# Turning eight probability tiles in float32 instead of as two float16 parts

## The chip, the cores and the metric

One core of a Trainium2 chip. The metric is the device time of one execution in microseconds, as the median over runs.

## The reference

Three layers follow each other, for 2 batches of 768 positions. All inputs are float32.

```python
# 1: attention inside hash buckets, 8 heads of 64
mask = q_bucket[:, :, :, None] == k_bucket[:, :, None, :]
scores = np.where(mask, scale * np.matmul(q, k.transpose(0, 1, 3, 2)), -1e9)
attn = np.exp(scores - scores.max(-1, keepdims=True))
attn = attn / (attn.sum(-1, keepdims=True) + 1e-09)
x = np.matmul(attn, v)            # -> (2, 768, 512)
# 2: four causal attention experts of width 64, the best two weighted
for e in range(E):
    a = softmax(causal(scale * (x @ wq[e]) @ (x @ wk[e]).T))
    out += weight_of(e) * (a @ (x @ wv[e]) @ wo[e])
# 3: mixing with the previous position, then a gated two-layer network
xk, xr = mu_k * x + (1 - mu_k) * x_prev, mu_r * x + (1 - mu_r) * x_prev
return sigmoid(xr @ w_r) * (np.maximum(xk @ w_k, 0.0) ** 2 @ w_v)
```

The buckets come from the signs of `q @ proj` and `k @ proj` (6 bits).

## The kernel before

The work is cut into 12 units i of 128 query positions (6 for each batch). A unit runs through the three layers: `lsh_steps` (layer 1, heads h = 0 to 7), `moe_steps` (layer 2), `mix_steps` (layer 3). In front of them stand the weights (`weight_steps`) and, for each batch, the keys and values (`key_steps`) and the queries (`query_steps`).

Products keep nearly float32 precision by splitting every operand into a float16 high part and a float16 rest, the low part, and adding three products. `hi_part` and `lo_part` make them: high is a rounding copy, low is source minus high. Splitting therefore takes work on DVE, ACT and POOL for every tile, weights included (the instructions named wm, wd, WK, WR, WV make the parts of the layer 3 weights from raw loads).

For one tile (i, h) of layer 1, `score` has PE write 128x768 scores s into PSUM. Then `softmax` runs: DVE copies the scores to P in SBUF and finds the row extreme (the instruction P<-s, with a small mx after it), ACT takes the exponential in place and the row sum, a high part PHL[:, :n] is made by ACT or POOL, a low part PHL[:, n:] by POOL. Both parts must be turned (positions of the keys onto the partitions) to PT before PE can multiply by the values v (the products named x). For 88 of the 96 tiles a DMA on SP's queue turns PHL as a whole. For the eight tiles in `SD`, units 0 to 3 with heads 0 and 3, PE does it: six 128x128 turns of the high part into one PSUM bank (tp0), six of the low part into another (tp1), and ACT evicts the one, DVE the other. Which engine makes the high part is counted in `hi_engine`: of each eight calls the first two go to POOL, the rest to ACT. Tiles of layer 2 call it too (132 calls in all).

Float32 turns exist in the kernel already: `turn32` turns x and y between the layers in float32, and splits them while PSUM is emptied, high on ACT, low on DVE.

Nothing runs in the order in which the code stands. `Program` records every call as an operation (consecutive calls of one step on PE are one), 2546 in all; `arrange` puts them into the order of the table `ORDER`, which a planner wrote, and the table `HOMES` gives each tile its buffer. Each engine and the DMA queue of SP then work through their part of that list in order, and wait by semaphores for what they need. All calls go through line 201, which is why each row of the profile bears it. PSUM has two buffers for scores (`ps_s`) and four single banks (`ps_d`) for all else, the turns among them.

Of the kernel before, what the change touches and what calls it, by code (L numbers as in the profile page):

```python
# [12 lines left out]
F16 = mybir.dt.float16  # L13
# [3 lines left out]
AF = mybir.ActivationFunctionType  # L17
# [6 lines left out]
SV = 64.0  # L24
# [14 lines left out]

QD, KD, XD, YD = (8, 9, 10, 11), (), (8, 9, 10, 11), (8, 9, 10, 11)  # L40
SD = {(i, h): "av" for i in range(4) for h in (0, 3)}

# [186 lines left out]
def tile_lsh_moe_mix(  # L229
# [14 lines left out]
    P = 128  # L244
# [83 lines left out]
    def turn(dst, src, nm, by_dma=False):  # L328

        if by_dma:  # L330
            nc.sync.dma_start_transpose(dst, src)
            return
        n = src.shape[1] // P
        hn = n // 2
        if n > 8:
            pt = [dps(f"tr_{nm}_{j}").bitcast(F16)[:, :hn * P] for j in range(2)]
        else:
            pt = dps(f"tr_{nm}").bitcast(F16)
            pt = [pt[:, j * hn * P:(j + 1) * hn * P] for j in range(2)]
        for j in range(2):  # L340
            for c in range(hn):
                nc.tensor.transpose(pt[j][:, c * P:(c + 1) * P], src[:, (j * hn + c) * P:(j * hn + c + 1) * P], ident16)
            nc.vector.tensor_copy(dst[:, j * hn:(j + 1) * hn, :], pt[j].rearrange("p (n s) -> p n s", s=P))
# [100 lines left out]
    def key_steps(b, g):  # L444
# [11 lines left out]
        def half(j):  # L456
            if j == 0:
# [13 lines left out]
                 na.rearrange("p h t c -> p (h t c)"), f"y2_{nm}_{j}", (b, g) in KD)  # L471

        def hash_():
# [4 lines left out]
            for j in range(2):  # L478
                turn(st["y1"][:, 2 * j:2 * j + 2].rearrange("p h (t s) -> p (h t) s", s=P),
                     st["nb"][j].rearrange("p h t c -> p (h t c)"), f"y1_{nm}_{j}", (b, g) in KD)  # L480
# [17 lines left out]
    def query_steps(i):  # L498
# [4 lines left out]
        def prep():  # L503
# [9 lines left out]
            turn(x2, na.rearrange("p h c -> p (h c)"), f"x2_{i}", i in QD)  # L513

        def hash_():
# [4 lines left out]
            turn(x1, nb.rearrange("p h c -> p (h c)"), f"x1_{i}", i in QD)  # L520
# [19 lines left out]
    def hi_engine():  # L540
        NS[0] += 1
        return "p" if (NS[0] - 1) % 8 < 2 else "a"

    def softmax(Sv, n, scale, sm, bias, nm, masked=None, by_pe=None):
# [3 lines left out]
        PHL = sp.tile([P, 2 * S], F16, tag="b3", bufs=NB3, name=f"PHL_{nm}")[:, :2 * n]  # L548
# [456 lines left out]
```

## Time and profile before

| | |
|---|---|
| median of 3 runs | 470.1 us (467.38 to 470.42) |
| the profiled execution | 470.66 us, its span 468.9 us |
| mean granted TensorE clock | 0.981 |
| PE busy | 428.9 us, 91% of the span |
| DVE, ACT, POOL busy | 345.3, 345.0, 324.2 us |

The span goes from the first to the last instruction. Engines: PE is TensorE's matrix product, PEld its weight load, DVE is VectorE, ACT ScalarE, POOL GpSimd, SP the queue that issues most DMAs. A row of a group names what an instruction writes, an arrow, and what it reads; buffer numbers are left out, so that PHL stands for all PHL tiles of layer 1. Idle time before a group is given with what ended it.

### The profile page before, as it was taken

The page shows a single profiled execution, that of the slowest core. Times are in us where ns is not written, and L with a number is a line of the kernel's source. Part 1 is how long each engine was busy: PE and PEld are TensorE (multiplying, and loading weights), DVE is VectorE, ACT ScalarE, POOL GpSimd, SP SyncE. Part 2 cuts the span into 40 slices and gives each one's busy share as a digit, 9 for nine tenths or more (in the row PEclk, how much of TensorE's full clock was granted, in tenths as well). Part 3 has the DMA queues.
Part 4 walks back from the last instruction along what each step waited for, and adds up shares of the span by engine and source line. Part 5 has one row for each costly group of instructions (what it writes and reads, how often), then busy time and mean ns, then how long its engine had stood idle before and what let it go on. Part 6 is the DMA issues. An engine that isn't in the chain of part 4 may idle for free.

```text
span 468.9 us, 15555 instructions
## 1 busy us (share of the span) xinstructions
PE 428.9 (91%) x6296; PEld 328.6 (70%) x6296; DVE 345.3 (74%) x970; ACT 345.0 (74%) x654; POOL 324.2 (69%) x321
## 2 busy tenths in 40 slices
PE   2965679899899999998999999999999999999996
PEld 1843467677777779787777778687668769867572
DVE  3999989989999779899695667955768644643421
ACT  4369889979999889777985977878777975543320
POOL 5579899879886977876989468857766945362000
PEclk9997889989999999999999999999999999999999
DMA  8978989899999999989999799978998894555101
GB/s 228 284 191 194 198 191 180 171 225 170 181 219 199 204 178 192 191 157 181 164 184 170 158 148 150 179 148 141 141 156 119 140 187 82 126 81 125 46 24 45
DMA packets 227160, 75.59 MB, mean 161 GB/s; under 512 B 218512, under 2 KB 222736, under 8 KB 227088
## 3 DMA queue, kind: packets, MB, share of 16 engines
q1 hardware_dynamic: 225584, 74.48, 85.4%
q8 instruction: 49, 0.80, 0.7%
q10 hardware_dynamic: 1504, 0.11, 0.2%
q14 instruction: 23, 0.19, 0.1%
HBM read 22.14 MB, written 3.15 MB: 54 GB/s over the span
## 4 chain that ended last, share of the span: by engine, by line
PE 61%; DVE 11%; POOL 10%; DMA 8%; issue 6%; ACT 4%; SPq 0%; POOLq 0%; DVEq 0%; ACTq 0%
PE v L201 12%; PE h L201 11%; PE x L201 7%; PE s L201 7%; POOL PHL L201 6%; PE r L201 5%; PE qk L201 5%; DVE P L201 3%; DMA PT<-PHL 3%; PE se L201 3%; PE y L201 3%; PE o L201 3%; PE tr_y L201 2%; PE vg L201 2%; DMA PT_m<-PHL_m 1%
## 5 line engine op out<-in xcount | busy, mean ns | idle before, releaser
L201 POOL TENSOR_TENSOR PHL<-P,PHL 128x768 f16<-128x768 f32 x96 | 159.7, 1672 | 36.1 <-ACT PHL L201 34.4
L201 DVE TENSOR_SCALAR_CACHE_REDUCE P<-s 128x768 f32<-128x768 f32 x96 | 91.0, 951 | 19.1 <-PE s L201 12.7
L201 ACT ACTIVATE P<-P,mx 128x768 f32<-128x768 f32 x96 | 89.1, 928 | 16.3 <-DVE mx L201 15.7
L201 PE MATMUL s<-y,x 128*128 128x384 f16 x384 | 80.7, 336 | 8.7 <-DVE P L201 6.1
L201 PE MATMUL h<-mk,WK 128*128 128x128 f16 x1152 | 72.6, 219 | 0.0
L201 PEld LDWEIGHTS <-WK 128*128 128x128 f16 x1152 | 67.0, 98 | 4.0
L201 PE MATMUL x<-v,PT 128*128 128x64 f16 x1728 | 64.3, 195 | 2.1 <-DVE v L201 2.0
L201 PEld LDWEIGHTS <-PT 128*128 128x128 f16 x1728 | 60.2, 99 | 6.8 <-issue 2.4
L201 ACT ACTIVATE PHL<-P 128x768 f16<-128x768 f32 x72 | 59.9, 839 | 4.9 <-DMA PT<-PHL 1.6
L201 PEld LDWEIGHTS <-x 128*128 128x128 f16 x576 | 40.8, 99 | 28.8 <-issue 10.1
L201 PE MATMUL v<-WV,k2h 128*128 128x512 f16 x192 | 57.1, 379 | 0.0
L201 POOL TENSOR_TENSOR PHL_m<-P_m,PHL_m 128x512 f16<-128x512 f32 (+2 forms) x24 | 34.3, 1429 | 18.6 <-ACT PHL_m L201 10.2
L201 PE MATMUL qk<-xT,WQK 128*128 128x128 f16 x576 | 35.8, 219 | 1.0 <-DVE xT L201 0.5
L201 PE MATMUL v<-WV,k2l 128*128 128x512 f16 x96 | 36.4, 379 | 0.0
L201 PEld LDWEIGHTS <-WQK 128*128 128x128 f16 x576 | 33.1, 98 | 2.6 <-DMA xT<-hl_x 0.9
L201 PE MATMUL r<-WR,mr 128*128 128x512 f16 x144 | 34.5, 379 | 0.0
L201 DVE SCALAR_TENSOR_TENSOR h<-h,t 128x512 f32<-128x512 f32 x24 | 16.6, 694 | 20.7 <-ACT t L201 20.7
L201 ACT ACTIVATE t<-h 128x512 f32<-128x512 f32 x24 | 14.2, 590 | 23.4 <-PE h L201 23.3
L201 DVE TENSOR_SCALAR_CACHE_REDUCE P_m<-se 128x512 f32<-128x512 f32 (+2 forms) x24 | 19.6, 818 | 13.4 <-PE se L201 3.8
L201 PEld LDWEIGHTS <-k2h 128*128 128x128 f16 x192 | 17.0, 98 | 13.2 <-issue 0.2
L201 POOL TENSOR_SCALAR PHL<-P 128x768 f16<-128x768 f32 x24 | 21.0, 876 | 7.5 <-ACT P L201 3.5
L201 ACT ACTIVATE P_m<-P_m,bias_m 128x512 f32<-128x512 f32 (+2 forms) x24 | 19.7, 821 | 7.8 <-DVE P_m L201 7.7
(143 smaller groups left out, 867.8 us busy)
## 6 DMA issues: line engine op xcount, KB each, us to landing
raw_k<-in_moe_w_k_dram SPq DMA_DIRECT2D x8, 512.0 KB, 4.5
raw_v<-in_moe_w_v_dram SPq DMA_DIRECT2D x8, 512.0 KB, 4.3
q<-in_q_dram SPq DMA_DIRECT2D x12, 256.0 KB, 5.3
k<-in_k_dram SPq DMA_DIRECT2D x8, 384.0 KB, 5.2
v<-in_v_dram SPq DMA_DIRECT2D x8, 384.0 KB, 4.7
out_dram<-e SPq DMA_DIRECT2D x12, 256.0 KB, 2.6
raw_r<-in_moe_w_r_dram SPq DMA_DIRECT2D x4, 512.0 KB, 4.5
PT<-PHL SPq DMA_TRANSPOSE x88, 4.3
```

Source lines behind the costliest of these rows:

```text
L201: getattr(getattr(self.nc, engine), method)(*[real(a) for a in args], **{k: real(a) for k, a in kw.items()})
```

## The change

```diff
+def HP(n):
+    return n % 8 < 2
...
     def hi_engine():
         NS[0] += 1
-        return "p" if (NS[0] - 1) % 8 < 2 else "a"
+        return "p" if HP(NS[0] - 1) else "a"
...
         nc.scalar.activation(Pt, Pt, AF.Exp, bias=bias, scale=-scale if masked else -1.0, accum_out=sm)
+        if by_pe:
+            nk = n // P
+            hn = nk // 2
+            for j in range(2):
+                pt = dps(f"tp{j}_{nm}", [P, hn, P])
+                for c in range(hn):
+                    nc.tensor.transpose(pt[:, c], Pt[:, (j * hn + c) * P:(j * hn + c + 1) * P], ident32)
+                hi, lo = (PT[:, a * nk + j * hn:a * nk + (j + 1) * hn, :] for a in range(2))
+                hi_part("a", hi, pt)
+                lo_part("v", lo, pt, hi)
+            return PT
+        PHL = sp.tile([P, 2 * S], F16, tag="b3", bufs=NB3, name=f"PHL_{nm}")[:, :2 * n]
         hi_part(hi_engine(), PHL[:, :n], Pt)
         lo_part("p", PHL[:, n:], Pt, PHL[:, :n])
-        if by_pe:
-            nk = n // P
-            for j, eng in enumerate(by_pe):
-                pt = dps(f"tp{j}_{nm}").bitcast(F16)[:, :n]
-                for c in range(nk):
-                    nc.tensor.transpose(pt[:, c * P:(c + 1) * P], PHL[:, j * n + c * P:j * n + (c + 1) * P], ident16)
-                o = PT[:, j * nk:(j + 1) * nk, :]
-                pt = pt.rearrange("p (t s) -> p t s", s=P)
-                if eng == "a":
-                    nc.scalar.activation(o, pt, AF.Copy)
-                else:
-                    nc.vector.tensor_copy(o, pt)
-            return PT
         nc.sync.dma_start_transpose(PT, PHL)
         return PT
```

For the eight tiles P itself is turned in float32: three 128x128 turns into one PSUM bank, three into another. As each bank is emptied, ACT writes the high part (128x384) into PT and DVE the low part, PSUM minus high. The PHL tile and its two instructions are gone for these tiles. `turn` also gets an argument for the engine that evicts, and two tables KE and QE that are empty, so that it does as before; HP has the old rule.

Two things follow that no line of the diff says. The eight tiles no longer count in `hi_engine` (124 calls instead of 132), so that the two-in-eight rule falls on other tiles behind them. And both tables are new: `ORDER` again holds 2546 numbers, since six operations of a tile take the place of six, but only 67 of them stand at the place they had; `HOMES` has 1283 entries for 1291, the eight PHL tiles being gone. Decoded and read by name, the new order begins with other work: SP issues the first key load in front of all, and the two small operations on prhl come on DVE behind three splits of keys and queries, no longer first. Ahead of PE's first product h of layer 3 (h_0_0), DVE's list has 220 operations instead of 216, POOL's 88 instead of 93, ACT's 134 as before.

## Rows read from the trace of the kernel before

**Rows 1.** The page's first part: busy us, share of the span, instructions.

```profile
PE 428.9 (91%) x6296; PEld 328.6 (70%) x6296; DVE 345.3 (74%) x970; ACT 345.0 (74%) x654; POOL 324.2 (69%) x321
```

**Rows 2.** Busy time by stretch: from:to, length, engines' busy us, clock, DMA.

```profile
core 0: us, PE busy (x) PEld busy (x) DVE busy (x) ACT busy (x) POOL busy (x), PEclk, DMA share, GB/s
...
15.00:110.00 95.00, 73.77 (x1091) 58.21 (x1089) 89.15 (x240) 78.00 (x151) 81.90 (x83) 0.91 0.92 198
110.00:150.00 40.00, 38.16 (x582) 29.38 (x577) 38.54 (x114) 38.43 (x76) 34.52 (x35) 1.00 0.99 195
30.00:45.00 15.00, 8.32 (x88) 5.70 (x88) 14.37 (x33) 14.23 (x27) 14.68 (x15) 0.87 0.85 196
45.00:60.00 15.00, 11.12 (x137) 7.86 (x135) 13.87 (x29) 13.47 (x25) 13.07 (x12) 0.78 0.88 182
60.00:75.00 15.00, 12.06 (x197) 10.29 (x195) 13.96 (x35) 12.20 (x23) 14.42 (x12) 0.89 0.89 176
150.00:450.00 300.00, 296.73 (x4480) 228.75 (x4481) 204.82 (x599) 219.32 (x416) 199.90 (x191) 1.00 0.87 148
```

**Rows 3.** The chain that ended last, 20 to 135 us: start, duration, what.

```profile
33.24 1.62 POOL PHL L201
...
38.25 1.50 POOL PHL L201
...
39.83 2.22 POOL PHL L201
...
49.90 0.87 DVE P L201 x2
...
51.23 1.75 DVE P L201 x4
...
100.02 3.25 POOL PHL L201 x2
```

**Rows 4.** Groups by form, whole span: instruction, count, busy us, mean ns, idle before.

```profile
L201 POOL TENSOR_TENSOR PHL<-P,PHL 128x768 f16<-128x768 f32 x96 | 159.7, 1672 | 36.1 <-ACT PHL L201 34.4
...
L201 ACT ACTIVATE PHL<-P 128x768 f16<-128x768 f32 x72 | 59.9, 839 | 4.9 <-DMA PT<-PHL 1.6 <-issue 1.1 <-PE y L201 0.4
...
L201 POOL TENSOR_SCALAR PHL<-P 128x768 f16<-128x768 f32 x24 | 21.0, 876 | 7.5 <-ACT P L201 3.5 <-PE x L201 1.8 <-issue 1.3
...
L201 PE MATMUL tp<-consts,PHL 128*128 128x128 f16 x96 | 9.3, 241 | 1.1 <-ACT wd_v L201 1.0
...
L201 ACT ACTIVATE PT<-tp 128x768 f16<-128x768 f16 x8 | 6.4, 802 | 0.5 <-PE tp L201 0.5
...
L201 DVE TENSOR_TENSOR xT<-tr_x,xT 128x512 f16<-128x512 f32 x8 | 5.5, 686 | 0.8 <-ACT xT L201 0.8
...
L201 PE MATMUL tr_x<-ident,x 128*128 128x128 f32 x32 | 5.4, 296 | 0.3 <-DVE mx L201 0.3
...
L201 ACT ACTIVATE xT<-tr_x 128x512 f16<-128x512 f32 x8 | 4.8, 596 | 1.4 <-PE tr_x L201 1.2
...
L201 DVE COPY PT<-tp 128x768 f16<-128x768 f16 x8 | 4.4, 552 | 1.3 <-PE tp L201 1.3
...
L201 DVE TENSOR_TENSOR yT<-tr_y,yT 128x256 f16<-128x256 f32 x8 | 3.3, 417 | 0.0
...
L201 ACT ACTIVATE yT<-tr_y 128x256 f16<-128x256 f32 x8 | 3.0, 373 | 0.8 <-PE tr_y L201 0.8
```

**Rows 5.** Groups by form on DVE, 15 to 150 us.

```profile
L201 DVE SCALAR_TENSOR_TENSOR v<-v,v 128x768 f16<-128x768 f32 x4 | 5.8, 1456 | 0.0
...
L201 DVE SCALAR_TENSOR_TENSOR nak<-k,nak 128x768 f16<-128x768 f32 x1 | 0.9, 945 | 0.0
```

**Rows 6.** Instructions in order of time: start, duration, instruction, idle before it.

```profile
7.07 0.55 DVE L201 CAST prhl<-pr 128x6 f16<-128x6 f32 x1 [7.07 <-DMA pr<-in_proj_dram]
...
7.65 0.17 DVE L201 TENSOR_TENSOR prhl<-pr,prhl 128x6 f16<-128x6 f32 x1
...
42.07 1.44 PE L201 MATMUL s<-y,x 128*128 128x384 f16 x4 [4.29 <-DVE P L201]
...
110.53 0.66 PE L201 MATMUL h<-mk,WK 128*128 128x128 f16 x9
```

More of the change, by code (lines that the diff above doesn't have):

```diff
@@ L326, in mark, with turn @@
         nc.vector.tensor_scalar(dst[:, :, NB:], z, 0.0, OKV, op0=two, op1=OP.mult)
-    def turn(dst, src, nm, by_dma=False):
+    def turn(dst, src, nm, by_dma=False, engs="vv"):
         if by_dma:
@@ L342, in turn @@
                 nc.tensor.transpose(pt[j][:, c * P:(c + 1) * P], src[:, (j * hn + c) * P:(j * hn + c + 1) * P], ident16)
-            nc.vector.tensor_copy(dst[:, j * hn:(j + 1) * hn, :], pt[j].rearrange("p (n s) -> p n s", s=P))
+            o, pj = dst[:, j * hn:(j + 1) * hn, :], pt[j].rearrange("p (n s) -> p n s", s=P)
+            if engs[j] == "a":
+                nc.scalar.activation(o, pj, AF.Copy)
+            else:
+                nc.vector.tensor_copy(o, pj)
     def turn32(dst, src, n, nm, by_dma=False):
@@ L512, in prep @@
             st["x2"] = x2 = sp.tile([P, H, P], F16, tag="b2", bufs=NB2, name=f"x2_{i}")
-            turn(x2, na.rearrange("p h c -> p (h c)"), f"x2_{i}", i in QD)
+            turn(x2, na.rearrange("p h c -> p (h c)"), f"x2_{i}", i in QD, QE.get(i, "vv"))
         def hash_():
@@ L519, in hash_ @@
             st["x1"] = x1 = sp.tile([P, H, P], F16, tag="b2", bufs=NB2, name=f"x1_{i}")
-            turn(x1, nb.rearrange("p h c -> p (h c)"), f"x1_{i}", i in QD)
+            turn(x1, nb.rearrange("p h c -> p (h c)"), f"x1_{i}", i in QD, QE.get(i, "vv"))
         QS_[i] = [once(prep), once(hash_)]
@@ new lines @@
+8}8CW1$YGO+;mqF9zz}2;L1W#NDFo0sN3j{xq)tw>+LE*W$5mfxnCe5MDh*b2|R`4E}hE&86gpDa=*d}R|PV`aGx2LyU2c+CtnVdKz&FGiJ^~M;gZ2-7saz5
+<wy9&FxrpwE1meLe!g4iqWK$e6Mln{t}0}KVlc+Pgt5MdTi~MmThIhnxmU2ry@qjqvFpZLoO<&kT=37}IjnXK;UAdj8^I+1FI0o3u*RMBzr$^~;O@Y9zr_6k
+f8(F9)s1p}-Cbw~&EcH?4<`6~@B!|_WZwcl!Y7E~BlvCZ0sMf6aNaL<+udLA0$RaV|2MRTxV{avgl&F@D~NC4GrWa&;QU1gz7Xzoqg`8Q4_{!3kK?EKU2eN?
+2OZ#~D~hrFcNhYNajB2zr~08V9G3ZFSOhQl9sWJ^0rW@xSm*s$_z8x=2)N`%!Z-LC`om>+%rEyHVHBKlEBs1-+FfyHTo>pIXWd*M)9>{WeQZAfuDX6O5YD-I
+KECe;<J@_7&2@)C&;yS91im<4ccWpaAMd)tMZe46bA#cgCiJU)CrIQk`5UeT?(?0YCnWa0pd=>uWpEsfhh)AKuJOI$gum%-xe0LFmBqDwnm_4x`#CVio$~ix
@@ new lines @@
+Y25E8LQ>xW$G})f;_tY1{(w*AAGj3$uA2lMaWeda4_!H&0#jjvn+DTi1~~c;N8o&)+COqB{SO2>=vVp6{<QDT3;bhu$S?GZ{475cX2EP2iPQZPH^a~NPu&}r
+#;5h=aTLz<bD<O7^yz&D-x<5$a>(v;_&GkK&*U@vEPe^x@)fWv=JXZujKAvB`DIWaZ}<k7%P)njejdz+hPV(8`^A2}?}54f2EWPY_t*VKzu7m!Eq*U8fJ(T>
+KXd<LHecPpb(QhCTLf49HNO~o;yahekH#@r1z)&c_}&%pA6!BI(H-%(ePe8bdHq;SrQPrsw;I;M8mNjjuo}K}h5RR19c$tp?+K|EzH+_st}pCY!2o>inqod5
+4aVU;Pc#r~V>5i<nSOQa;5WAcgnoDH;l5Ye2u2V6BVPyWVi8}|mykbPbL@jF;IV(|OZeyhPxs6Z!YBTf|I78oK*f9nD(z#y3qKg6!#;ZB-}-lc2)_28`~)oS
+bJJ)4+4aMr7?EPad;ik6zz@ER|KcWNNngqzr2P~NzWTEMi*JdsVHnoKzuf^U=i|UH{&#<f^3bn-IDYeA-8Wa>PsCQ(9g|R8ibUUiYpme&QX4!>75x<a?tb%s
@@ new lines @@
+_&<GHoP_N#DfP#nyoaBCKFUvj`M>>7?kF9hsd$2-QF}~A$tf}&qj+?j;!|`wN&mQyekD}#<FT@@<Wti{s_OrB2`C0l!=K%Bj7c-Fn*YyTq94w|CfE#_X$x$H
+05h=wMWKYW4PsFuLU0IB!`Je)eNA7-H}HTBy~lzSm3G2**abV_hyTz2<Nx&pDJTmy^7TCfqCi&K4Rw8EzXue0awJSi^?U?~O-+0nN=y6U01zI8XLO1V0pn#d
+5Znv<;54P8#MD*d&``cYnJD04h=7Gju`HFMBVZU2(ouSf1U)!1WT2}Q1+GyMiV8(3BNd`-RE#3xT%3)wa1Iuy5|o{C&;p!?k?{;Yrxz3l=VL5fh*9w+y`rO#
+i;h7wJPvDdGe*JKSdwy5FW!NDxHs>^z8oE2(^)!4TW~9urbW0IoB48dp59PgT#7q!KW@Y2*xdg?OK=^Qq3yT~cj0>6fCq2|uEc}55f9-FYU*3~@>GFVVMY3r
+R^v^Ifh~O{s!Xl?H|obn@ILLvJ-7xp;a+U*tI%;A!2P+6KY@QyU1~tXxSI^;aXilcrhlj&HKb!WkOy;He;C{O_Wmfw#75MZn$RGAKuzf(J)&kbgm2Mps!tc_
@@ new lines @@
+I*sQJeiWa?Q#hLcr4c-l|D*GK8mrR;?k;!eE=}Uc^n@<s7_Lgys0MZP?`SfAr=MsnkGC^;7Hd;Y`kCrbEpmJjFW_5xPakLsf265=4$tE!x<|*jv%iF$Jn~oS
+>bv+Blv;nGZayAf;O_nk-bLaYcpI6g@pZh1J^ZiqnV!;b)RKDoJ9v?=VJm7)$N2=O(W}_Y_x8WjP5eU5sfV<ok=)1k_5FN*Kfqt(fxaDm;6eU6d!EiSc^04M
+vwVhU^9(-6z$f`We&j1WkLU1ezRZ{S6nCbpJfG)sI&Dim=>~t|n|z0F@onxx8~F!4<|llgdrMFGm+$f|ZBHGjBXy!))SLRyE$m9&s5`~SzVwzKa3AR<n^<@=
+-{b%I2PeXWm;gWXLtem%aSLzd9<+@g@fRLMUwI*KXD1-z$V(D@%8Pgj_or{16yLG(Gk(rXc`^UW{b(Tdl^tySonP=8UdMs^OEUb8m+^8=j{W4e{?3s(0!QR1
+yn<hH3LHQ&I1=yYl$Z)r<4=t8Gq2=7_)q?e*YZvtOhafFzvopPjd$|_9!k+UD#zx7{5QYiG`NRN67wJ#AR@2%uBPN9e25QoOn!iIIUeujv>KoH@exkSaX1+t
@@ new lines @@
+<>Z_dv*BO~GEgGO8&1brI02{E44P5X^LkFjsd)ouQkCquK+<pq&dLiV7ANGim;uw_5MdccL**Y{A?cB1I1Q6UGF%o*MjRn4B`v4m!XX=H=aG_#Gjb-*!6WDw
+jwq{Sv^3Wi+ER1iC>leVFf(SsRvJk*$Vke?k!7{C)+n-3#z;;cE1M)Q=i|{dmd4WznqX_Bjjol<JWAT?I?2zQCAvhD2{f5z(sY_cIWZUJ#ypr8C(<-361K=V
+nJJkyhRl-LGG4aIHi;_<B#|VRB(g*%$WqCrc{n%Ek))DEKVnoVz%eDO#*%CrTXJi5ohZvBhrYx2_!2+hE1V>+@eS^fcrsT$VI294ljSWYl$|m~zTj6(A&2BK
+u9t`S1Rvo&Jt*^}B+r+rGEH*oBuggK<&N%>8In>`OMH2X&#{C)!;+duALwq`BQNm2KGgkEUJpn?uAucbuQt$cm_e4ycl-%|#_jS8{))fh@0dnXNg=MN8Kp26
+;f9)7lFMG%C)M?^eAgpVG?db`l1{QnCOIm3B(LO?Kk%4T(yWqR@@Zvlq}e39<ku?NSPN)XZKB1vhSt=d^te>hqWp*ElulYuPsm9r&bcIqG}WK=Pt7g)rH~fZ
@@ L951 @@
+y3ZOn
 """
 HOMES = """
[L954 to L957 removed]
@@ L962 @@
+${I&)5OrAxG0A1Y8uzo>hyT@EQE1k2aVtsSg!oDKqv+M9r<mBR9S`}V2=R!TMcE*VQ<MM1gOD?t6wg{*HoQAY$mJkSHgyzrJILq46&{*Cx3aQMPwsYloi8}M
+k3wZXw%Id6k&CLFKA3jvzA#yGd!Be_Syz?H>fQ<>E1RV6XOxTeE3Q2*Sjue1yZ-~t=pN?
 """
```

84 lines of the change are left out of this document (28 added, 56 removed).

## The prediction

> **What bounds the kernel now.** I read the page's engine shares first, then the busy time by stretch, then the chain of work that ended last, then the groups of instructions by form. The shares [rows 1] put TensorE (PE) far ahead: 428.9 of 468.9 us, with VectorE (DVE), ScalarE (ACT) and GpSimd (POOL) level near 74%. The stretches [rows 2] show where this average misleads. From 150 to 450 us PE is busy 296.73 of 300 us at full clock: what another engine saves there is worth nothing. From 15 to 110 us PE is busy only 73.77 of 95 us, and its granted clock is 0.91 (0.78 between 45 and 60 us). That stretch ends where PE gets its first hidden product h, at 110.53 us [rows 6]; from then on it has projection work to fill holes with, and from 110 to 150 us it stands idle 1.8 us only. All eight tiles of the change lie before 133 us, so the time is decided between the start and about 110 us. If that stretch becomes x us shorter, the kernel does.
>
> Who bounds that stretch? DVE is busy 89.15 of its 95 us: 5.85 us idle. POOL has 13.1 us idle, ACT 17.0. But the chain [rows 3] is not DVE's alone. Between 33 and 42 us, and again from 99 to 103, it runs through POOL's PHL instructions; from 49 to 53 us it runs through DVE's score reductions P. By the list of POOL's instructions these POOL pieces are: the low part of tile 0_3 (33.24), the high and low parts of tile 0_0 (38.25 and 39.83), and at 100.02 the low parts of 2_5 and 2_3. Three of the eight tiles thus stand on the chain: 1.62 + 1.50 + 2.22 + half of 3.25 = 7.0 us. So POOL holds the chain in places, but an engine with 5.85 us of slack stands right behind it.
>
> **The change part by part.** Prices are those of [rows 4].
>
> *POOL.* Eight low parts go: 8 x 1.672 = 13.4 us. The eight tiles also leave the count in hi_engine: 34 high parts of 132 ran on POOL, 32 of 124 will. Two of the eight were on POOL (0_0 and 3_3); of the others six tiles of 768 go to POOL and four of 768 and two of 256 leave it, the small ones at about half price. Together 13.4 + 6 x 0.876 + 0.8 - 6 x 0.876 = 14.2 us less.
>
> *ACT.* Six high parts (839 ns) and eight evictions (802 ns) go: 11.5 us. Sixteen high parts of 128x384 from PSUM come. No such row exists; it lies between 128x256 (373 ns) and 128x512 (596 ns), halfway 485 ns: 7.8 us. With the swap of engines above (0.8 us less) ACT has 4.5 us less.
>
> *DVE.* Eight evictions go (552 ns, 4.4 us), and sixteen low parts of 128x384 come, PSUM and one SBUF operand in. Rows of the same kind are 417 ns (128x256) and 686 ns (128x512), halfway 552: 8.8 us. DVE, the fullest engine, gets 4.4 us more.
>
> *PE.* 96 turns in float16 at 97 ns of busy time each (9.3 of 96) against 48 in float32 at 169 ns (5.4 of 32): 9.3 against 8.1 us. I take 0, since the turns lie where PE has 21.2 us of idle time for cover; without that cover the bounds are -1.2 and, with each float32 turn at its whole 296 ns, +4.9 us.
>
> *Order, buffers, DMA.* 88 tiles went by DMA and 88 will. The queue of SP keeps its 215 entries, in another order. Each turned tile held two PSUM banks for one eviction each (0.55 or 0.80 us); now each bank waits for ACT, then DVE, about 1.04 us. If PE always stood behind that, it would cost up to 16 x 0.24 to 0.49 = 3.8 to 7.8 us; with the second bank of the same tile free to fill, and PE idle anyway, I take 0. The eight PHL buffers are no longer asked for: a gain from 0 up to the waits they cause, taken as 0.
>
> The path inside one tile gets shorter: after the exponential came 0.84 (high), 1.67 (low), then turns and eviction; now turns, 0.49 and 0.55. That frees the x products of the eight tiles some 2 us earlier, which counts only where PE waits for these tiles and not for DVE.
>
> *What DVE has to do first.* The new order, decoded, tells how much of the 4.4 us falls before the point that matters. Ahead of the first h product DVE's list has 220 entries for 216. Thirteen low parts are new (7.2 us) and six evictions gone (3.3); behind the product have moved one wd instruction and one WV2 split (0.69 us each, as the 128x512 row) and one 256-wide reduction (0.42, as the 128x256 row). That is +2.1 us. Lower bound 0 (the planner moves more work than the list tells), upper 4.4 (all of it counts).
>
> *What DVE gains.* Its 5.85 us of idle time in the stretch is where POOL, PE and ACT were late. POOL loses 14.2 us of work there and ACT 4.5, so some of it closes: from 0 to 5.85, I take half, 2.9.
>
> *Stretched instructions.* The v split of DVE took 1456 ns on average in 15 to 150 us, while the nak split of the same form and size took 945 in the same window [rows 5]; the four v splits run while POOL is nearly full [rows 2]. Excess: 4 x 0.51 = 2.0 us. POOL will be busy some 12% less (14.2 of 116.4 us between 15 and 150), so about 0.2 us comes back. The Trainium skill (GPSIMD Engine Reference, section 1, Specifications) says that GpSimd shares its SBUF interfaces with VectorE, and that the contention is with VectorE instructions that have two SBUF inputs or run in a two-port mode; the two rows agree with it. By that rule the new low parts, which read one operand from PSUM, would not be stretched, and if they were stretched as the v split is, they would cost 16 x 0.30 = 4.8 us more. The rows of xT and yT, which are such low parts, bear the unstretched price [rows 4].
>
> *The start.* DVE's first instruction waits 7.07 us for the small table pr [rows 6], and 0.72 us goes to prhl before any key. In the new order SP issues the keys first and prhl comes behind three key and query splits. I take -0.7 us, between -1.5 and 0.
>
> **The sum.** -0.7 + 2.1 - 2.9 - 0.2 = -1.7 us, that is 470.66 - 1.7 = 469.0 for an execution like the profiled one. That one lay 0.56 above the median of 470.1; the median becomes 468.4, in round figures **468**, a change of -0.4%.
>
> **The rivals.**
>
> *POOL, not DVE, held the stretch (faster).* Then the 7.0 us of the eight tiles on the chain go, with what ACT loses behind them, and DVE fills all its idle time: -0.7 - 5.85 + 2.1 = -4.5 by DVE's limit, or down to -0.7 - 7.0 = -7.7 where the chain's pieces go whole because DVE work is put later than the list tells. Around 464. For it: the chain; a POOL that is 14.68 of 15 us full from 30 to 45 us. Against it: DVE is 14.37 of 15 full there too, so that POOL's gain meets DVE after 0.6 us.
>
> *DVE pays everything, at one place (slower).* PE's longest hole, 4.29 us before 42.07 [rows 6], ended when DVE began to reduce scores again: ten DVE entries without a reduction lay in between, among them two v splits and one eviction. In the new list there are fifteen between two reductions at that place (tiles 0_3 and 0_2), with three v splits and both low parts of 0_3. That is one more v split (1.46) and 0.55 for the low parts, with the small ones some 3 us more, with both score buffers full and PE waiting. Behind that hole the clock was granted at 0.78 for 15 us, against 0.89 in the next 15 [rows 2]: on average 56% and 78% of that time at 2.4 GHz, the rest at 1.2. Another 15 us like it cost some 1.7 us. With 4.4 us of DVE work unpaid by any closed idle time: 470.1 + 4.4 + 1.7 = 476. If DVE does in this block only what it would have done anyway, the 3 us come back later; the rival decides if the first h product is later than about 114 us.
>
> *Nothing reaches the end.* POOL's gain is slack, DVE's 2.1 us are hidden behind closed waits: 470. This is the upper side of the forecast and is counted with it.
>
> **How the numbers follow.** What a measurement of this kernel can tell from no change is about 1%, 4.7 us. The forecast with its neighbour at 470: 0.5, own range 465.5 to 474. POOL as the holder: 0.3, around 464. DVE pays: 0.2, around 476. The range of 8 in 10 reaches from 461 (470.1 - 7.7 is 462.4, and one more for the clock) to 476. Faster by over 1% (below 465.4) 0.3, within 1% 0.5, slower (above 474.8) 0.2.
>
> **What will show it.** In the changed profile: 16 PT low parts on DVE near 552 ns and 16 high parts on ACT near 485; POOL at 310 us, DVE at 350, ACT at 340; first h product near 108.5 us (forecast), before 106 (first rival), after 114 (second). DVE's idle time between 15 us and that product falls to about 3 us. From 150 us on the two kernels should run alike; if the difference arises there, or in a longer tail after the last v product, the prediction is wrong in kind. It would also be wrong if the clock's low stretch near 45 us disappeared, which I give no chance of its own.

## The result, and the profile after

The changed kernel takes 472.41 us (median of 20 runs, 468.61 to 474.44), the kernel before 467.52 us on the same chip (20 runs, 464.08 to 470.75). The ratio is 1.0101, 95% interval 1.0079 to 1.0124: 1.0% or 4.9 us slower, where 0.4% faster was forecast.

The two profiled executions hide this. That of before took 470.66 us and stands at the upper end of its 20 runs; that of after took 470.13 us and stands near the lower end of its own. Laid side by side they show the changed kernel ahead by half a microsecond. Executions of one program differ here by more than the effect, so every reading below that rests on few microseconds is taken over several executions.

The first line of the page of after, engine by engine, answers to [rows 1]: busy us, share of the span, instructions.

```profile
PE 429.8 (92%) x6248; PEld 327.7 (70%) x6248; DVE 348.7 (74%) x978; ACT 343.7 (73%) x658; POOL 308.3 (66%) x311
```

DVE has 3.4 us more than in [rows 1], ACT 1.3 less, POOL 15.9 less. The new instructions, by form, on DVE, ACT and PE, answer to [rows 4]: count, busy us, mean ns, idle before.

```profile
L207 DVE TENSOR_TENSOR PT<-tp,PT 128x384 f16<-128x384 f32 x16 | 8.5, 545 | 0.0
...
L207 ACT ACTIVATE PT<-tp 128x384 f16<-128x384 f32 x16 | 7.4, 482 | 1.7 <-PE tp L207 0.9 <-issue 0.6
...
L207 PE MATMUL tp<-ident,P 128*128 128x128 f32 x48 | 8.9, 296 | 1.6 <-ACT P L207 0.8 <-ACT naq L207 0.4 <-DVE x L207 0.4
```

The busy time by stretch of after answers to [rows 2]: from:to, length, engines' busy us, clock, DMA.

```profile
core 0: us, PE busy (x) PEld busy (x) DVE busy (x) ACT busy (x) POOL busy (x), PEclk, DMA share, GB/s
15.00:110.00 95.00, 74.33 (x1069) 56.71 (x1067) 90.76 (x249) 75.05 (x153) 68.80 (x76) 0.89 0.90 198
110.00:150.00 40.00, 38.54 (x571) 29.82 (x571) 39.74 (x117) 38.05 (x77) 32.56 (x34) 1.00 1.05 202
...
150.00:450.00 300.00, 296.94 (x4440) 227.37 (x4437) 206.95 (x599) 222.24 (x419) 198.73 (x191) 1.00 0.87 148
```

POOL fell from 81.90 to 68.80 us in the first stretch, DVE went from 89.15 to 90.76. The same row of a second execution of the kernel before (464.76 us in all) shows how little the 89.15 is worth:

```profile
15.00:110.00 95.00, 73.27 (x1148) 57.78 (x1146) 92.31 (x252) 82.53 (x162) 86.52 (x87) 0.96 0.99 209
```

There DVE is idle 2.69 us and not 5.85. The table puts together all profiled executions whose program is, up to the first v product, that of before or that of after (their names are those of the experiments), and two, old_then_new and new_then_old, where it is so up to the first h product and beyond 110 us: first h product and first v product on PE from the list in order of time, and DVE's idle time from 15 to 110 us.

| program up to there | execution | first h, us | first v, us | DVE idle, us |
|---|---|---|---|---|
| before | first profile | 110.53 | 146.20 | 5.85 |
| before | look_before | 105.71 | 141.48 | 2.69 |
| before | old_to_200 | 107.95 | 143.36 | 3.75 |
| before | old_then_new_late | 106.06 | 141.74 | 2.77 |
| before | old_then_new | 109.15 | – | 4.57 |
| after | first profile | 109.09 | 145.32 | 4.24 |
| after | look_after | 109.41 | 147.07 | 3.92 |
| after | after_again | 109.02 | 146.31 | 3.58 |
| after | new_to_200 | 110.47 | 146.70 | 4.95 |
| after | new_then_old_late | 109.45 | 145.42 | 4.21 |
| after | new_then_old | 107.31 | – | 2.57 |

The medians are 108.0, 142.6 and 3.8 us for before, 109.3, 146.3 and 4.1 for after. So the changed kernel comes 1.3 us later to the first h product, which is uncertain by some 2 us, and 3.8 us later to the first v product, and DVE does not stand idle less. From the first v product to the end of the span the two executions of before took 322.7 and 321.4 us, the three of the changed kernel 323.0, 325.7 and 324.6. By these executions most of the loss stands behind the first h product. The profile on which the prediction was built is the latest of its five.

### The profile page after: what moved, and what is told of

Same layout as the page of the kernel before. It is cut to its first block, busy times and chain, and to the rows that moved or that the text cites. A ratio compares the mean times of both kernels' runs of the same rounds, so it can differ in the third digit from the quotient of the medians.

```text
span 468.3 us, 15437 instructions
## 1 busy us (share of the span) xinstructions
PE 429.8 (92%) x6248; PEld 327.7 (70%) x6248; DVE 348.7 (74%) x978; ACT 343.7 (73%) x658; POOL 308.3 (66%) x311
## 5 line engine op out<-in xcount | busy, mean ns | idle before, releaser
L207 POOL TENSOR_TENSOR PHL<-P,PHL 128x768 f16<-128x768 f32 x88 | 144.4, 1650 | 33.4 <-ACT PHL L207 30.3
L207 DVE TENSOR_SCALAR_CACHE_REDUCE P<-s 128x768 f32<-128x768 f32 x96 | 91.0, 950 | 20.0 <-PE s L207 13.1
L207 ACT ACTIVATE PHL<-P 128x768 f16<-128x768 f32 x64 | 53.2, 838 | 4.7 <-DMA PT_m<-PHL_m 1.0
L207 PE MATMUL qk<-xT,WQK 128*128 128x128 f16 x576 | 36.9, 219 | 1.6 <-DVE k2l L207 0.9
L207 PE MATMUL r<-WR,mr 128*128 128x512 f16 x144 | 35.8, 379 | 0.0
L207 POOL TENSOR_TENSOR mk<-m32k,mk 128x512 f16<-128x512 f32 x12 | 13.9, 1160 | 21.6 <-PE h L207 12.1
L207 ACT ACT_TABLE_LOAD x18 | 23.1, 1283 | 5.4 <-issue 2.9
L207 PE MATMUL o<-yT,WO 128*128 128x128 f16 x288 | 22.2, 222 | 2.2 <-DVE mx L207 1.1
```

What stands on the lines that cost most here:

```text
L207: getattr(getattr(self.nc, engine), method)(*[real(a) for a in args], **{k: real(a) for k, a in kw.items()})
```

## The experiments

**Both kernels profiled once more.**

> The kernel before, once more, for a second profile: the first one (470.66 us) lay 3 us above the median of 467.5. Every theory expects about 467; what is asked is where a usual execution differs from the first profile between 15 and 110 us (PE's holes, the stretch of low clock), and whether PE's first h product comes nearer to 107 than to 110.5 us.

> The changed kernel, once more, for a second profile: the first one (470.13 us) lay 2.3 us below the median of 472.4. Theory 1 (DVE bounds the stretch up to the first h product and pays for the low parts): first h product 2 to 5 us later than in a usual execution of the kernel before, DVE's idle time in 15 to 110 us under 5 us. Theory 2 (the new order costs, not the operations): the loss stands in places where no tile of the eight is near, at the start (constants late, PE's first product at 8 us) or behind 150 us.

They took 464.76 and 474.64 us. The rows above come from them: what differs between two executions of before arises ahead of the first h product (4.8 of 5.9 us), and from the first v product to the end of the span they agree within 1.3 us (322.7 and 321.4). look_after bears out something of both theories: its first h product, at 109.41 us, comes later than in four of the five executions of before, and its 325.7 us behind the first v product are more than in either execution of before.

**The new operations in the old order.** The turns stand where the old turns stood, the high and low parts where the evictions stood, all else as before but for four buffers.

```diff
 # one tile's entries in the lists, at their old places
-POOL/ACT high, POOL low, PE turn 0, ACT eviction 0, PE turn 1, DVE eviction 1
+PE turn 0, ACT high 0, DVE low 0, PE turn 1, ACT high 1, DVE low 1
```

> The new operations in the old order: turns, high and low parts of the eight tiles stand where their turns and evictions stood, all other operations and engines as before. Theory 1 (DVE's 4.4 us more are paid): slower than before by 3 to 5 us, ratio 1.006 to 1.011. Theory 2 (the new order costs): ratio 0.995 to 1.003, since POOL has 13 us less and nothing else moved.

482.37 us, ratio 1.0322 (1.0284 to 1.0361): 15 us lost, more than either theory expected. The first h product came at 116.92 us. DVE's waits from 15 to 150 us:

```profile
DVE PT L207 <- ACT PT L207: 7.0, 6, 2.1
DVE wd_v L207 <- ACT wd_v L207: 1.8, 1, 1.8
```

The second low part stood right behind ACT's high part, and ACT was late: DVE, the fullest engine, waited 7.0 us for it. PE's waits before score products came to 8.9 us, against 6.1 and 7.1 in the two executions of before. Where the rest of the 15 us goes was not traced. The new order of the changed kernel is thus part of what makes the change bearable. In that order this wait is small: 0.8 us, once, in after_again.

**4.4 us more on DVE in the old program, and 4.4 us less.** Both evictions of the eight tiles on DVE, or both on ACT; one letter differs.

```diff
-SD = {(i, h): "av" for i in range(4) for h in (0, 3)}
+SD = {(i, h): "vv" for i in range(4) for h in (0, 3)}   # sd_aa: "aa"
```

> The kernel before, with both evictions of the eight tiles on DVE instead of one on ACT: DVE gets 8 x 0.552 = 4.4 us more, as much as the change gives it, ACT 6.4 us less; order, PE and POOL as before. Theory 1: slower by 3 to 5 us, ratio 1.006 to 1.011. Theory 2: no change, 0.998 to 1.003.

> The kernel before with both evictions of the eight tiles on ScalarE (eight moved from VectorE: VectorE 4.4 us less, ScalarE 6.4 us more), the counterpart of the run with both on VectorE, which was 1.0005. If VectorE alone set the pace, this is faster: 0.992 to 0.996. If ScalarE's list is the tighter one for work put into it, slower: 1.004 to 1.010; then the run with both on VectorE was a trade of 4.4 us more there against 6.4 less on ScalarE and did not show that VectorE's time is free.

sd_vv: 468.25 us, ratio 1.0005 (0.9975 to 1.0035). sd_aa: 468.51 us, 1.0016 (0.9994 to 1.0038). Neither moves the time beyond its interval, which reaches to 1.6 and 1.8 us slower; sd_aa fell between its two expectations. Since each is a trade (4.4 us of DVE against 6.4 of ACT), they do not show that DVE's time is free; they show that in the old program the lists of the two engines can give and take this much, to within these intervals. In sd_vv DVE was idle only 1.88 us of the 95:

```profile
15.00:110.00 95.00, 71.99 (x1144) 56.61 (x1141) 93.12 (x253) 77.21 (x150) 86.25 (x87) 0.96 0.96 204
```

So an engine can look all but full here and still have taken work at no cost beyond the interval.

**The late constants.** In after, PE's first turn waits for the constants, which are third in ACT's queue, and DVE behind it:

```profile
7.97 1.44 PE L207 MATMUL tr_y<-consts,nak 128*128 128x128 f16 x12 [7.97 <-DMA consts<-in_consts_dram]
...
8.81 1.20 DVE L207 COPY y<-tr_y 128x768 f16<-128x768 f16 x2 [2.78 <-PE tr_y L207]
```

```diff
 # ORDER, ACT's queue
-pr32, ties, consts, mur, ...
+consts, pr32, ties, mur, ...
```

> The changed kernel with one transfer moved: that of the constants goes out as the first of ScalarE's queue instead of the third. In the changed kernel TensorE's first turn waited for it until 7.97 us while its input was ready at 6.1. If the late start is carried to the end: 470.5 us (1.9 us less), ratio about 1.006. If VectorE's list closes up behind it, as most single delays of the first 60 us seem to be closed: 472.0, ratio 1.009 to 1.011.

PE's first turn came at 6.08 us, and the time stayed: 471.31 us, ratio 1.0102 (1.0068 to 1.0137).

```profile
6.08 1.46 PE L207 MATMUL tr_y<-consts,nak 128*128 128x128 f16 x12 [6.08 <-DVE nak L207]
```

No gain from a start 1.9 us earlier is seen at the end; the interval, which reaches 1.6 us to either side, would not show a part of it.

**Zeros in place of the low parts.**

```diff
-                lo_part("v", lo, pt, hi)
+                nc.gpsimd.memset(lo, 0.0)
```

> The changed kernel, in its order, with the low parts of the eight tiles left out: GpSimd fills them with zeros instead, so VectorE has 16 subtractions (8.5 us) less and never waits for ScalarE's high parts; the eight tiles' turned probabilities lack their low halves. If VectorE's work and its wait for the high part are the cost: 464 us or less (467.5 of before less the 4.4 us of evictions that it had there, 463 to 466), ratio 0.990 to 0.997. If the float32 turns on TensorE or the new order are the cost: 471 to 472.4, ratio 1.007 to 1.011.

470.44 us, 1.0090 (1.0060 to 1.0119). This run cannot tell: POOL wrote the zeros late, and PE waited for them instead.

```profile
PE x L207 <- POOL PT L207: 2.0, 1, 2.0
```

**The low parts gone altogether.**

```diff
-                lo_part("v", lo, pt, hi)
...
+                lo = ident16 if (i, h) in SD else PT[:, NT + t, :]
-                nc.tensor.matmul(o, PT[:, NT + t, :], kg["v"][:, 0, hh, t, :], start=False, stop=(t == NT - 1))
+                nc.tensor.matmul(o, lo, kg["v"][:, 0, hh, t, :], start=False, stop=(t == NT - 1))
```

> The changed kernel with the 16 low parts of the eight tiles gone altogether (nothing stands in their place on any engine; the x products of those tiles read the identity matrix in their place, so these products are not the reference's). VectorE has 8.7 us less, TensorE the same. If VectorE's work up to the first v product is what costs, all or most of the 8.7 us comes off: 464 to 466 us where the changed kernel has 472, ratio 0.992 to 0.997. If the order of the rest or the float32 turns cost, it stays at 1.006 to 1.010. In the run before, zeros written by GpSimd came late at one product (2.0 us), so that run could not tell.

469.14 us (12 runs), 1.0031 (1.0011 to 1.0050). Against the 1.0101 of the changed kernel, 0.70% or 3.3 us come back: not the whole 8.7 us, but most of the loss, and a ratio between the two expectations. The first h product comes at 107.20 us, 2.1 us ahead of the median of after, the first v product at 144.59:

```profile
107.20 0.22 PE L207 MATMUL h<-mk,WK 128*128 128x128 f16 x1
...
144.59 0.60 PE L207 MATMUL v<-WV,k2h 128*128 128x512 f16 x2
```

**Copies in place of the low parts.** The same tiles out, at the same place in the list, with nothing needed of ACT.

```diff
-                lo_part("v", lo, pt, hi)
+                nc.vector.tensor_copy(lo, pt)
```

> The changed kernel with the 16 low parts on VectorE turned into plain copies from PSUM (the same tiles, the same place in the list, 128x384 out), so that they need nothing of ScalarE's high parts; the eight tiles' low parts are not the reference's. Leaving them out gave 1.0031 where the changed kernel has 1.0101. If VectorE's time is what they cost: 1.009 to 1.011 here. If it is that VectorE stands behind ScalarE: 1.003 to 1.005, and no wait of VectorE for ScalarE's PT is left.

472.80 us, 1.0111 (1.0081 to 1.0141): the loss is all there again. DVE's group by form, and then its wait for ACT from 15 to 150 us:

```profile
L207 DVE CAST PT<-tp 128x384 f16<-128x384 f32 x16 | 8.5, 549 | 1.1 <-ACT PT L207 1.1
```

```profile
DVE PT L207 <- ACT PT L207: 1.1, 1, 1.1
```

The copies take as long as the subtractions did (549 and 545 ns). One wait that the profile puts down to ACT's PT is still there, so the edit did not clear it; but at 1.1 us here, and 0.8 in after_again, it is too small for the 3.3 us. So it costs that DVE has sixteen instructions of this length at these places, whatever they compute. Which way the cost goes is not separated: in after PE waited once 1.2 us for a bank that a low part held, and once 0.8 us for a low part before an x product, and lo_unused takes these waits away too (the first is from PE's waits, the second from its list in order of time):

```profile
PE tr_x L207 <- DVE PT L207: 1.2, 1, 1.2
```

```profile
43.41 0.50 PE L207 MATMUL x<-v,PT 128*128 128x64 f16 x6 [0.78 <-DVE PT L207]
```

**Half of the query evictions of units 0 to 3 to ACT.** This takes 3.3 us off DVE, by the hook that the change brought.

```diff
-KE, QE = {}, {}
+KE, QE = {}, {i: "va" for i in range(4)}
```

> The changed kernel with eight of the first four units' query turns (one half of each) emptied by ScalarE instead of VectorE, at their places in the lists: VectorE 3.3 us less, ScalarE some 5 us more, nothing left out. If VectorE's load is the cost: ratio 1.003 to 1.005 (2.5 us less than the changed kernel). If it is the order, or if ScalarE's list is just as full: 1.009 to 1.014.

480.39 us, 1.0271 (1.0237 to 1.0304): 8 us slower than the changed kernel, outside both expectations. What the waits show is not a list of ACT that is too long, but that a moved eviction stands where ACT comes to it before PE has made the turn. ACT's waits from 15 to 110 us:

```profile
ACT x L207 <- PE tr_x L207: 16.8, 6, 6.4
ACT x L207 <- DVE x L207: 6.0, 1, 6.0
```

ACT stood 22.8 us before the moved evictions, and DVE, relieved, was busy 79.56 of the 95 us.

**Eight more high parts to POOL,** which had 26 us of idle time in that stretch.

```diff
 def HP(n):
-    return n % 8 < 2
+    return n % 8 < 2 or n < 32 and n % 8 in (2, 5)
```

> The changed kernel with eight more high parts of the first four units (two of each, SBUF to SBUF, 128x768) made by GpSimd instead of ScalarE, at their places in the lists: ScalarE 6.7 us less, GpSimd some 6.7 us more, of which it was busy only 69 of the 95 us from 15 to 110. Eight evictions moved onto ScalarE cost 8 us; if ScalarE's list is as tight as VectorE's there, taking eight instructions off it gives 2 to 4 us: ratio 1.003 to 1.007. If GpSimd's room is of no use because its parts come one behind the other and the tiles' transfers then leave later: 1.010 to 1.014.

478.53 us, 1.0227 (1.0198 to 1.0256): 5 us slower than the changed kernel, outside both expectations. POOL stands before its new instructions, and DVE behind POOL (the waits of POOL, then those of DVE, 15 to 110 us):

```profile
POOL PHL L207 <- ACT P L207: 7.9, 2, 7.5
```

```profile
DVE P L207 <- POOL PHL L207: 2.8, 1, 2.8
DVE vg L207 <- POOL gt L207: 2.0, 1, 2.0
```

**Which part of the new order costs.** The two programs have the same number of operations, one for one, so one can run the first part of the one and the rest of the other (order and buffers). The cut was tried at three places. At operations 873 and 1221 the two programs stand some operations apart:

> The changed kernel with its own program up to a cut between its first h and its first v product (operation 873 of 2546), and from there the order and the buffers of the kernel before. All new turns and splits lie ahead of the cut. If all that was lost is lost where the new turns stand, it takes the time of the changed kernel, 472.4 us (471.5 to 473.5, ratio to before 1.009 to 1.012). If the part behind the first v, which in the profiles so far is 321.4, 322.7 and 323.2 us in three executions with the old order and 323.0 and 325.7 with the new one, is longer because of the order alone, it gains that back: 470.2 us (469.5 to 471), ratio about 1.006.

> The other half: the kernel before, with its own operations and order up to the same cut, and from there the order and buffers of the changed kernel; no operation is new in it. If the order behind the cut costs nothing: 467.5 us, ratio 0.998 to 1.002. If it costs what the two profiles of the changed kernel suggest: 469.8 us (469 to 470.5), ratio about 1.005. The gain of the run above and the loss of this one should be equal if the two halves add up.

> The changed kernel up to operation 1221 of 2546 (about 200 us), then the order and buffers of the kernel before: the cut is moved away from the stretch where the cuts at the first v product made x products wait for their turned tiles. If the loss lies ahead of 200 us: ratio 1.008 to 1.011. If half of it lies behind: 1.004 to 1.006.

> The kernel before up to the same operation, then the order and buffers of the changed kernel; no new operation. If the loss lies ahead of 200 us: 0.998 to 1.002. If half of it lies behind, in the order alone: 1.004 to 1.006.

new_then_old 471.75 us, 1.0124 (1.0099 to 1.0149); old_then_new 470.72 us, 1.0092 (1.0058 to 1.0125); new_to_200 471.41 us, 1.0084 (1.0053 to 1.0115); old_to_200 470.93 us, 1.0079 (1.0049 to 1.0110). Both halves of each pair lose, together 2.16% and 1.63%, more than the 1.0 to 1.2% of the change. The cut itself adds to it: PE waits right behind it. These are waits of PE in old_then_new (146 to 170 us) and, in the second fence, in old_to_200 (195 to 250 us):

```profile
PE x L201 <- DMA PT<-PHL: 3.0, 2, 2.2
```

```profile
PE s L201 <- DVE P_m L201: 2.8, 1, 2.8
```

What each half costs is not read from these four. At operation 1354 the two programs have done the same but for one product and one turn (by the count of PE's instructions this is near 222 us):

> The kernel before up to operation 1354 of 2546 and from there the order and buffers of the changed kernel. At this place the two programs have done the same operations but for one product and one turn, so the cut itself moves nothing; the cuts at 873 and 1221 each made TensorE wait 1.9 to 3.0 us at the cut. If those cuts were the loss there: 0.999 to 1.003. If the later part of the new order loses of itself: 1.005 to 1.008.

> The changed kernel up to the same operation and then the order and buffers of the kernel before. If the loss lies ahead of the cut: 1.008 to 1.011, as the changed kernel. If the later part of the new order loses of itself: 1.003 to 1.006. This ratio and that of the run before this one, added, should give that of the changed kernel in this call, if the cut is free.

> The changed kernel itself once more, on the chip of the three runs above, so that they can be set against it and not only against the kernel before: 1.008 to 1.012 by its first 20 runs.

old_then_new_late 468.54 us (12 runs), 1.0027 (1.0005 to 1.0050); new_then_old_late 470.96 us (9 runs), 1.0067 (1.0034 to 1.0099); the changed kernel itself, measured beside them, 472.80 us, 1.0119 (1.0089 to 1.0149). The two parts now add up, 0.27% and 0.67% to 0.94%, inside the interval of the whole. So some 3.1 us are lost ahead of about 222 us, where all new operations are, and some 1.3 us behind it, where no operation is new. The whole less the first part gives 2.4 us for the part behind, uncertain by some 2. PE's waits there in after_again, 330 us to the end, where look_before shows none:

```profile
PE qk L207 <- DMA xT<-hl_x: 1.1, 1, 1.1
PE o L207 <- DMA yT<-hl_y: 0.6, 1, 0.6
PE se L207 <- DVE qT L207: 0.4, 1, 0.4
```

The first profile of before also had a wait for xT (0.5 us), and old_then_new_late, which runs the new order there, has only the last of the three (0.4 us). So these 2.1 us are not what the order alone costs.

One thing more differs behind 222 us. ACT runs 18 ACT_TABLE_LOAD where before it ran 16, in every profile with the new order there and in none with the old. The groups of before and after, and ACT's list of after_again:

```profile
L201 ACT ACT_TABLE_LOAD x16 | 20.5, 1283 | 3.4 <-issue 3.1
...
L207 ACT ACT_TABLE_LOAD x18 | 23.1, 1283 | 5.4 <-issue 2.9 <-DVE mx L207 2.3
```

```profile
374.38 0.60 ACT L207 ACTIVATE e<-r 128x512 f32<-128x512 f32 x1 [0.34 <-PE r L207]
377.23 1.28 ACT L207 ACT_TABLE_LOAD   x1 [2.26 <-DVE mx L207]
378.53 0.94 ACT L207 ACTIVATE P<-P,mx 128x768 f32<-128x768 f32 x1
...
380.50 1.28 ACT L207 ACT_TABLE_LOAD   x1
381.79 0.60 ACT L207 ACTIVATE e<-r 128x512 f32<-128x512 f32 x1
```

The new order puts an exponential (P) between two sigmoids (e) that follow each other directly in before, and one more load of 1.28 us stands ahead of the exponential and one ahead of the second sigmoid. Whether the end comes later by it was not tested.

No version that came out of this beats the kernel before.

## Why the prediction was wrong

**The prices of the new operations were right.** High part 485 ns forecast, 482 measured; low part 552 and 545; POOL 310 and 308.3 us, DVE 350 and 348.7. ACT came to 343.7 us instead of 340; 2.6 of the 3.7 are the two table loads, which the prediction did not see in the new order. PE was taken as unchanged; its turns, forecast at 8.1 us, took 8.9, against 9.3 [rows 4] and 8.3 in the two executions of before.

**The start (-0.7).** DVE did begin earlier, at 5.07 us instead of 7.07 [rows 6], but then waited 2.78 us for PE, which waited for the constants. In consts_first the 1.9 us at the start changed the ratio by 0.0001, with an interval of 1.6 us to either side. No run shows the term.

**DVE's added work ahead of the first h product (+2.1).** It is there, at about half the size: from 15 us to that product DVE was busy 88.0 to 89.7 us in the five executions of before and 89.7 to 90.5 in the six of after, 1.1 us more in the median. The runs that reach further give more: 3.3 us by lo_unused, which takes away all sixteen low parts, 3.1 us by new_then_old_late for all that lies ahead of 222 us, both uncertain by about 1.5 us.

**Half of DVE's idle time closes (-2.9).** This is the step that failed. Its reason was that POOL loses 14.2 us. POOL lost 15.9, and DVE's idle time did not shrink: 4.1 us in the median against 3.8 before. Two mistakes went into it. The 5.85 us came from one execution, the latest of the five now known; in the others 2.69 to 4.57 us were there to close. And what is to close is only what POOL held. These are DVE's waits for POOL from 15 to 110 us in the first profile of before (0.6 to 1.4 us in the other four, none in the six of after), and then its two largest in the first profile of after, of which the first is new:

```profile
DVE wd_k L201 <- POOL wm_k L201: 1.8, 2, 1.4
...
DVE P L201 <- POOL PHL L201: 0.3, 1, 0.3
```

```profile
DVE x L207 <- PE tr_x L207: 2.1, 4, 0.8
DVE P L207 <- PE s L207: 1.8, 4, 0.6
```

So POOL's part did go, and in its place DVE waits for PE's turns of the queries and for scores. POOL itself stands idle because the work it follows comes late, and relieved, it stands idle longer: 26.2 us of the 95 in after, 13.1 before. Two of its waits there, in after:

```profile
POOL PHL L207 <- ACT PHL L207: 5.4, 3, 3.9
...
POOL gt L207 <- DVE lg L207: 3.6, 1, 3.6
```

Behind that stretch, in after_again, it stands idle from 126.97 to 135.12 us, but for one instruction:

```profile
126.30 0.67 POOL L207 TENSOR_SCALAR wm_v<-raw_v 128x512 f32<-128x512 f32 x1
129.64 1.65 POOL L207 TENSOR_TENSOR PHL_m_p<-P_m_p,PHL_m_p 128x768 f16<-128x768 f32 x1 [2.68 <-DMA PT<-PHL]
135.12 0.83 POOL L207 TENSOR_SCALAR PHL<-P 128x768 f16<-128x768 f32 x1 [3.84 <-DMA raw_v<-in_moe_w_v_dram]
...
129.76 0.70 PE L207 MATMUL x<-v,PT 128*128 128x64 f16 x18 [1.52 <-DMA PT<-PHL]
```

By this profile it waits for the transfer of a turned tile and for a weight load (the other two profiles of the changed kernel put the first of these waits down to ACT's high part), and at the same time PE waits 1.52 us for a turned tile. What shortens the DVE list's holes is an earlier arrival of what DVE waits for, and the change gave POOL time, not earlier inputs. Where POOL was given work for that time, it cost 5 us (hi_on_pool).

**The v splits (-0.2).** Their mean was 1198 ns in the first profile of after and 1424 in after_again, against 1456 and 1457 in before and 1236 in sd_vv. They vary between executions by more than the change could do, and not with POOL's load: POOL was busy 68.80, 68.63, 86.52 (look_before, 1457 ns) and 86.25 us (sd_vv) of the 95. What they vary with is what POOL runs at the moment. From the lists of POOL and DVE in after_again:

```profile
35.37 1.64 POOL L207 TENSOR_TENSOR PHL<-P,PHL 128x768 f16<-128x768 f32 x1
35.59 2.23 DVE L207 SCALAR_TENSOR_TENSOR v<-v,v 128x768 f16<-128x768 f32 x1
...
41.94 0.94 DVE L207 SCALAR_TENSOR_TENSOR v<-v,v 128x768 f16<-128x768 f32 x1
43.25 0.66 POOL L207 TENSOR_SCALAR wm_k<-raw_k 128x512 f32<-128x512 f32 x1 [3.16 <-DMA raw_k<-in_moe_w_k_dram]
```

The split at 41.94, with POOL idle, took 0.94 us. The one at 35.59 began when POOL's instruction had 1.42 us to go, and took 1.29 us longer. The 28 splits that seven profiles have between 15 and 150 us (before, look_before, sd_vv, after, look_after, after_again, lo_unused) all fit this: 0.94 us, and what the POOL instruction running or just begun had still to go, less about 0.1. The Trainium skill (GPSIMD Engine Reference, section 1, Specifications) lays such a stretch to the SBUF interfaces that GpSimd shares with VectorE; these lists agree with it. The low parts, with one operand in PSUM, took 541 to 558 ns in after_again, with or without a POOL instruction beside them, as that rule has it.

**Nothing behind the first h product (0).** This failed too, and the prediction had named it as an error in kind: 1.3 us (0.2 to 2.3) are lost behind 222 us by order alone. The stretch from the first h to the first v product is longer as well, 36.0 to 37.7 us in the five executions of after in the table against 35.4 to 35.8 in the four of before. The first profiles hide the late loss, with PE busy 296.73 us [rows 2] and 296.94 from 150 to 450 us; the second ones show it, with 297.91 in look_before, 294.84 in look_after and 295.96 in after_again.

By the medians the first h product comes some 1.3 us later (1.1 of DVE's work and 0.3 of its idle time) where the sum had it 1.7 us earlier, and the rest of the 4.9 us, some 3.6, is lost behind it, where the sum had nothing. Without the term for DVE's idle time the sum would have come to +1.2, slower.

**The rivals.** POOL as the holder falls: 13 us less on POOL in the deciding stretch did not bring the first h product forward. DVE paying everything had the right sign and, at 476, the wrong place and size: the hole of 4.29 us before a score product [rows 6] did not grow. At that place of after PE has several short waits instead:

```profile
36.18 0.61 PE L207 MATMUL tr_x<-consts,nbq 128*128 128x128 f16 x8 [1.74 <-DVE nbq L207]
...
42.11 0.52 PE L207 MATMUL x<-v,PT 128*128 128x64 f16 x12 [1.72 <-ACT PT L207]
...
44.29 2.74 PE L207 MATMUL s<-y,x 128*128 128x384 f16 x8 [0.37 <-DVE P L207]
```

The first h product came at 109, not after 114 us.

**What stays open.** 8.7 us fewer on DVE give 3.3 us in the new program; at that rate the 4.4 us more of sd_vv would cost 1.7 in the old one, where 1.0005 was measured and 1.6 us lie just inside the interval. So whether DVE's load costs less in the old program is not settled. That the place in the list counts is shown: the same new operations cost 1.0% in the one order and 3.2% in the other (ops_old_order). Which of the sixteen places costs is not shown. By what the late order costs, waits or table loads, was not tested by removing them.

## What to carry to other kernels

An idle time that is to be closed has to be read in several executions, and for each gap the question is what arrived late, not which engine had much to do: relieving an engine that itself waits for inputs only makes it wait longer. Where the order of every engine is written out, an instruction given to another engine at its old place can cost more than it weighs (8 evictions, 8 us; 8 high parts, 5 us), so a change is priced by places in lists and not by sums of busy time. Where the whole order is written anew, the sum has to cover all of it: by the profiled executions most of the loss stood behind the stretch that this one was made for. Two orders are compared by running one up to a point and the other behind it, but only at a point where both have done the same work; elsewhere the cut costs as much as the effect.

## What was not expected of the hardware

The same program reached its first h product at 105.71 us in one execution and at 110.53 in another. The rows of the shorter one (look_before), 45 to 75 us, beside those of [rows 2]:

```profile
45.00:60.00 15.00, 9.69 (x148) 6.88 (x146) 14.97 (x33) 13.47 (x25) 14.65 (x13) 0.95 0.93 194
60.00:75.00 15.00, 12.35 (x216) 10.52 (x217) 14.43 (x43) 14.34 (x28) 14.92 (x14) 1.00 1.05 220
```

The clock was granted at 0.95 and 1.00 there, against 0.78 and 0.89, and DVE and POOL were fuller. Both executions have the same hole of 4.29 us on PE ahead of it, which ends at 42.07 us in the one [rows 6] and at 40.85 us in the other. From 45 to 60 us PE was busy 11.12 us with 137 instructions in the longer execution and 9.69 us with 148 in the shorter, so its busy time is no measure of its work there. Whether the low clock is a cause of the later h product or goes with something else that differs, these runs do not tell. From the first v product on, where the clock is 1.00 in both, they agree within 1.3 us.
